# First loads split over two issuing engines, and attention's first two score tiles placed inside the last value unit

## The chip, the cores and the metric

The kernel runs on one core of a Trainium2 chip. The metric is the device time of one execution in microseconds (us); the lower the better. Three runs of the kernel before took 1822.64, 1822.76 and 1823.33 us, so the median is 1822.76. One more execution was profiled. The profile gives times from the first instruction's start and names engines: PE is the matrix engine (PEld its weight loads), DVE is VectorE, ACT is ScalarE, POOL is GpSimd, SP is SyncE, which here only issues DMAs. A "q" behind an engine's name means its issuing sequencer.

## The reference

With x of shape (1, 2048, 1024), 32 heads of 32 channels, and everything in 32-bit floats:

```
def _A_ref(x, wqkv, wo):
    q, k, v = split(x @ wqkv)                       # 32 heads, 32 channels
    p = softmax(einsum("bhqd,bhkd->bhqk", q, k) * 32 ** -0.5)
    return merge_heads(einsum("bhqk,bhkd->bhqd", p, v)) @ wo

def _B_ref(x, w_q, k1, k2, u, v):                   # 64 experts, the best one per head
    q1, q2 = halves(einsum("nd,dhc->nhc", x, w_q))
    e = argmax(q1 @ k1.T) * 8 + argmax(q2 @ k2.T)   # per token and head
    return sum over heads of gelu(x . u[e]) * v[e]  # the softmax over one candidate is 1

g = sigmoid((x * gate_w).sum(-1))
return g * _A_ref(x, wqkv, wo) + (1 - g) * _B_ref(x, w_q, k1, k2, u, v)
```

## The kernel before, in words

Large products run as sums of rounded parts: an operand is split into a high part (ACT copies it, rounded: `hi_of`, or line 95 of `split`) and a low part (DVE subtracts the high part from the operand: line 96), and three products, high by high, high by low and low by high, are summed. Most of them also use a scheme with seven block products P1 to P7 where plain blocks would need eight; one such product is 12 matmuls into one PSUM bank (four steps over the inner dimension, three pairs of parts each). PSUM has eight banks per core, called `bk0` to `bk7` here.

The stages follow each other on PE, whose order is the order of the code; no scheduler moves anything (`tc.manual_schedule()`), and every engine works through its own list in that order, waiting on semaphores where an operand or a buffer is not ready.

1. Queries and keys (0 to 364 us). The first 128 columns of keys and of queries for the first 1024 tokens are done plainly, in eight steps kc of 128 input channels, 12 matmuls each (`plain_mm`, line 291). Step kc needs 128 rows of x for 1024 tokens and 128 x 128 blocks of two weights, called A and S in the profile. The code calls the loads of weights `load_w0(k0, k1, queues)`: columns k0 to k1 in units of 128, one DMA for each of the two weights, each on the queue named. `load_x(p, kc, pieces)` loads the 128 rows of step kc in that many DMAs; the rows of steps 0 to 3 lie in the raw tile that the profile calls `xh`. Before the first step, eight matmuls of an identity tile (line 409) run on PE. After step 3 the gate's small products follow (line 191).
2. The router of the expert part (364 to 453 us).
3. Values. Two passes for the last four tiles of 128 tokens (453 to 497 us), and then six value units of two tiles each (`values_unit`, 497 to 615 us), each with the seven products; the last unit takes them in the order P1, P7, P5, P6, P3, P2, P4. DVE assembles the results: after P6 it does four adds in a row, u2 = c1 + P6, u3 = u2 + P7, u2 = u2 + P5, u5 = u3 + P5; after P3, u2 = u2 + P3; after P2, c1 = c1 + P2; after P4, u3 = u3 + P4. A bank is free once the last add that reads it is done. In the last unit the products lie in these banks: P1 bk6, P7 bk7, P5 bk0, P6 bk1, P3 bk2, P2 bk3; P4 goes to a bank `o` in a new pool that takes the place of bk7 once the eight banks' pool is closed.
4. Attention (615 to 1641 us). For each head and each tile kt of 128 keys, four matmuls of 512 queries each give scores in seven banks used in turn, the ring (line 1322); ACT writes exp of them to a tile P (line 1332); four matmuls with the values add to the head's output (line 1343). Tiles go in pairs: PE does the scores of one pair and then the value products of the pair before. DVE sums P over the tiles for the softmax's denominator; four tiles of a head (three of the last) are summed by accumulating DMAs of POOL instead, into a tile `accd` (`SUMS` names the tiles kt that do so; ACT writes the first of them straight into `accd`). The scores of head 0's first tile are taken out of this loop: `first_scores`, lines 1219 to 1229, issues them in the last value unit, between P2 and P4, into the banks bk5, bk6, bk0 and bk1, and exp of them (line 1229) follows on ACT.
5. The output product with the expert part added, and the stores (1641 to 1821 us).

DMAs that SP and ACT issue carry one of eight semaphores in turn, and an issue waits until the DMA before it with the same semaphore has landed.

Of the kernel before, what the change touches and what calls it, by code (L numbers as in the profile page):

```python
# [18 lines left out]
H = 32  # L19
# [12 lines left out]
def gated_mha_peer_kernel(ctx, tc, xT, wqkv, wv, wo, wq, k12, ug, v, out):  # L32
# [8 lines left out]
    nc = tc.nc  # L41
# [33 lines left out]
    def dma(dst, src, queue=nc.sync):  # L75
        a, b = (ap.bitcast(F32) if ap.dtype == F32R else ap for ap in (dst, src))
        return queue.dma_start(a, b)
# [92 lines left out]
    def load_x(p, kc, pieces=1):  # L170
        rows, t0 = slice(kc * 128, (kc + 1) * 128), TOK0[p]
        if kc < HC:
            n = 1024 // pieces
            for i in range(pieces):
                dma(XR["ra"][:, kc, i * n:(i + 1) * n], xT[rows, t0 + i * n:t0 + (i + 1) * n])
        else:
            for i, name in enumerate(("B21", "B22")):
                dma(XR[name][:, kc - HC, :], xT[rows, t0 + i * 512:t0 + (i + 1) * 512])
# [102 lines left out]
    b0, prod_no = {}, [0]  # L281
# [88 lines left out]
    def load_w0(k0, k1, queues=(nc.sync, nc.sync)):  # L370
        for w, queue in enumerate(queues):
            dma(w0[:, w, k0:k1], wqkv[w * 8, :, k0 * 128:k1 * 128].rearrange("p (k m) -> p k m", m=128),
                queue)

    def split_w0(k0, k1):
        ki, k = divmod(k0, HC)
        for w in range(2):
            hi, lo = AW[PLAIN[w, ki]]
            split(hi[:, k:k + k1 - k0], lo[:, k:k + k1 - k0], w0[:, w, k0:k1])
# [11 lines left out]
    for name in ("B11", "B12", "B21", "B22"):  # L391
        X[name] = x_parts(PASS[0][name], None, xp)

    load_w0(0, 1, (nc.scalar, nc.sync))
    load_x(0, 0, 2)
    load_w0(1, 2)
    load_x(0, 1)
    split_w0(0, 1)
    split_x(0)
    load_w0(2, 4)  # L400
# [264 lines left out]
    wl_, wh_, pools = [], [], []  # L665
# [239 lines left out]
    tp = Pool("tp", side="right")  # L905
# [64 lines left out]
    def tt(out, a, b, op=OP.add):  # L970
        nc.vector.tensor_tensor(out=out, in0=a, in1=b, op=op)
# [108 lines left out]
    def load_x_raw(u):  # L1080
        dma(x_raw[u % 2], xT[:, u * W:(u + 1) * W].rearrange("(k p) m -> p k m", p=128))
# [63 lines left out]
    def values_unit(u):  # L1145
        last = u == NU - 1
        c1, u2, u3, u5 = (work[k] for k in ("c1", "u2", "u3", "u5"))
        if last:
            free = x_raw[(u + 1) % 2].rearrange("p k m -> p (k m)").rearrange("p (a m) -> p a m", m=512)
            c1, u2, u3, u5 = (free[:, k] for k in range(4))  # L1150
        order = (("P1", "P2", "P3", "P7", "P5", "P6", "P4") if u == 0 else
                 ("P1", "P7", "P5", "P6", "P3", "P2", "P4") if last else
                 ("P1", "P7", "P5", "P6", "P2", "P3", "P4"))
        p, done = {}, set()

        def out(j, half, t, queue=nc.sync):
            dma(VD[half][(2 * u + j) * 128:(2 * u + j + 1) * 128, :], t, queue)

        for k, name in enumerate(order):
            if last and name == "P4":  # L1160

                nonlocal pso
                ps1.close()
                pso = Pool("pso", space=PSUM, side="right")
            p[name] = hv.product(name, bank=pv_bank if last and name == "P4" else None)
            if last and name == "P2":
                first_scores()
            if name == "P1":
                nc.scalar.activation(c1, p[name], AF.Copy)
                hv.rows(x_raw[(u + 1) % 2])  # L1170
                if u + 2 < NU:
                    load_x_raw(u + 2)
            if name == "P6":
                tt(u2, c1, p["P6"])
                tt(u3, u2, p["P7"])
                tt(u2, u2, p["P5"])
                tt(u5, u3, p["P5"])
                out(1, 1, u5)
            if "P6" in p:
                if "P2" in p and "C11" not in p:  # L1180
                    p["C11"] = tt(c1, c1, p["P2"])
                    out(0, 0, c1)
                if "P3" in p and "C12" not in p:
                    p["C12"] = tt(u2, u2, p["P3"])
                    out(0, 1, u2)
            if name == "P4":
                tt(u3, u3, p["P4"])

                out(1, 0, u3, nc.gpsimd if last else nc.sync)

            if u + 1 < NU:
                if k == (4 if u == 0 else 0):
                    hv.parts("A11")
                    for s in ("S3", "S1", "S2", "S4"):
                        hv.sums(s)
                    done = {"P1"}
                if k >= 5 or u > 0:
                    for q in ("P7", "P5", "P6", "P2", "P3", "P4"):
                        if q in p and q not in done:
                            hv.parts(hv.FACTORS[q][0])  # L1200
                            done.add(q)
            if 1 <= u <= HC:
                if k == 0:
                    load_early(u - 1)
                if k == 3:
                    sums_early()
                for j in {4: (0,), 5: (1,), 6: (2, 3)}.get(k, ()):
                    split_early(u - 1, j)

    P, pools = {}, {}  # L1210

    def p_tile(h, kt):

        i = pools["next"] % 8
        pools["next"] += 1
        P[h, kt] = pools["left" if i >= 4 else "right"].tile([128, S], F32, name=f"P{i}")
        return P[h, kt]

    def first_scores():

        tp.close()
        pools.update(right=Pool("ppr", side="right"), next=0)
        K, Q = Z
        pt = p_tile(0, 0)
        for qc, i in enumerate((5, 6, 0, 1)):
            ps = ps1.tile([128, 512], F32, name=f"bk{i}")
            c = slice(qc * 512, (qc + 1) * 512)
            nc.tensor.matmul(ps, K[:98, :128], Q[:98, c], start=True, stop=True)
            nc.scalar.activation(pt[:, c], ps, AF.Exp, scale=SCALE)

    def pv_bank():
# [49 lines left out]
    def ring_banks(n):  # L1281
        i = [(ring_no[0] + k) % NB for k in range(n)]
        ring_no[0] += n
        return i
# [26 lines left out]
    def scores(tiles):  # L1311


        n = NQ * len(tiles)
        banks = ring_banks(n)
        cuts = {1} | set(range(NQ, n + 1, NQ)) | {c for c in range(1, n) if banks[c] == 0}
        cuts |= {c + 2 for c in range(NQ, n, NQ) if not cuts & {c + 1, c + 3}}
        c0 = 0
        for c, i in enumerate(banks):
            (h, kt), qc = tiles[c // NQ], c % NQ  # L1320
            K, Q = KQ[h % 2]
            on_ring(nc.tensor.matmul(ring[:, i, :], K[:98, kt * 128:(kt + 1) * 128],  # L1322
                                     Q[:98, qc * 512:(qc + 1) * 512], start=True, stop=True), i)
            if c + 1 not in cuts:
                continue
            q0, m = c0 % NQ, c + 1 - c0
            if q0 == 0 and kt == SUMS[h == H - 1][0]:
                P[h, kt] = ACCD[h] = wk.tile([128, S], F32, name="accd")
            elif q0 == 0:
                p_tile(h, kt)  # L1330
            i -= m - 1
            on_ring(nc.scalar.activation(  # L1332
                P[h, kt][:, q0 * 512:(q0 + m) * 512].rearrange("p (a m) -> p a m", a=m),
                ring[:, i:i + m, :], AF.Exp, scale=SCALE), *range(i, i + m))
            c0 = c + 1
# [12 lines left out]

    SUMS = (1, 3, 8, 12), (2, 4, 6)

    def rowsum(ps, *srcs):
        for src in srcs:
# [3 lines left out]
                                       start=(src is srcs[0]), stop=(src is srcs[-1]))  # L1358

    def presum(h, kt):  # L1360
        sums = SUMS[h == H - 1]
        if kt == 0 or kt == sums[0] or (h == H - 1 and kt >= NT - 2):
            return
        if kt in sums:
            nc.gpsimd.dma_start(ACCD[h], P[h, kt], accum_op=OP.add)  # L1365
            return
        if kt == 1 + (sums[0] == 1):
            if h > 0:
                ACC[h] = wk.tile([128, S], F32, name="acc")
            nc.vector.tensor_add(ACC[h], P[h, 0], P[h, kt])  # L1370
        else:
            nc.vector.tensor_add(ACC[h], ACC[h], P[h, kt])  # L1372
# [97 lines left out]
    for k in range(2 * KC):  # L1470
        c = slice(k % 2 * D // 2, (k % 2 + 1) * D // 2)
# [10 lines left out]
    for b0 in range(0, (H + 1) * NT, BT):  # L1482
        if b0 > H * NT:
            break
        now = [divmod(k, NT) for k in range(b0, b0 + BT)] if b0 < H * NT else []
        if now:

            scores(now[b0 == 0:])
        for k in range(b0 - BT, b0):
            if k >= 0:  # L1490
                pv(*divmod(k, NT))
        for k in range(b0, b0 + BT):
            for f, a in todo.pop(k, []):
                f(*a)
            if now:
                presum(*now[k - b0])
# [278 lines left out]
```

## Time and profile before

| | |
|---|---|
| median of three runs | 1822.76 us |
| the profiled execution, whole | 1822.43 us |
| its span, first to last instruction | 1820.6 us |
| PE's granted clock | 1.0 of full speed |
| PE busy | 1813.5 us, 100% of the span |
| DVE, ACT, POOL busy | 1461.6, 1313.0, 227.7 us |
| DMA engines, mean | 190 GB/s |

A row of the timeline gives the start in us, the time from the first start to the last end of instructions merged into it, the engine and line, the operation, output<-inputs, the shape, and the count; a bracket at its end gives the engine's idle time before it and what ended it. A row of the table of waits gives who waited for whom, the total in us, how often, and the longest. A row of the chain of waits gives start, length, and what was done or waited for there. Ends of matmuls are modelled, so a matmul's length in these rows is longer than the distance to the next one's start; the text works with starts.

### The profile page before, as it was taken

The numbers are of one execution on the slowest core, as the hardware profiler recorded it, in microseconds if no ns is written. First come the engines' busy times: TensorE is split into PE (matmuls) and PEld (weight loads), VectorE is DVE, ScalarE is ACT, GpSimd is POOL, SyncE is SP. The second block draws the span as 40 slices with busy tenths as digits, with TensorE's granted clock in tenths as the row PEclk, the third lists the DMA queues.
The fourth block names the chain that finished last, engine by engine and source line by source line (L and its number), as shares of the span: only waits on it lengthen the run. The fifth ranks groups of instructions, "written<-read, shape, count | busy, mean of one in ns | idle before, by whom it ended". The sixth has DMA issues, their size and how long they took to land.

```text
span 1820.6 us, 26391 instructions
## 1 busy us (share of the span) xinstructions
PE 1813.5 (100%) x10077; PEld 1100.2 (60%) x10077; DVE 1461.6 (80%) x1258; ACT 1313.0 (72%) x1716; POOL 227.7 (13%) x351
## 2 busy tenths in 40 slices
PE   9999999999999999999999999999999999999999
PEld 6777777788888644444444444444444444447887
DVE  8865966789967888888888888888888888897674
ACT  6545544522333699999999999999999999994221
POOL 1222222244101100000000000000000000000000
PEclk9999999999999999999999999999999999999999
DMA  7888698660267778777778878888787778866641
GB/s 272 281 276 273 216 295 289 196 220 13 81 231 247 223 166 183 156 170 165 169 171 174 185 160 179 171 172 181 164 185 167 163 164 181 186 149 240 256 157 58
DMA packets 117072, 345.23 MB, mean 190 GB/s; under 512 B 16112, under 2 KB 49552, under 8 KB 96016
## 3 DMA queue, kind: packets, MB, share of 16 engines
q1 hardware_dynamic: 87752, 196.35, 36.6%
q0 software_dynamic: 27888, 145.00, 34.5%
q10 hardware_dynamic: 1304, 2.17, 0.3%
q8 instruction: 80, 1.31, 0.3%
q14 instruction: 48, 0.39, 0.1%
HBM read 171.76 MB, written 72.36 MB: 134 GB/s over the span
## 4 chain that ended last, share of the span: by engine, by line
PE 99%; DMA 0%; ACT 0%; SPq 0%; DVE 0%; issue 0%; DVEq 0%; ACTq 0%
PE ring L1322 29%; PE o L1343 26%; PE bk L303 15%; PE pa L965 6%; PE bk L965 6%; PE bk L726 5%; PE pa L1525 2%; PE bk L984 2%; PE bk L291 2%; PE bk L342 2%; PE ring L1356 1%; PE pa L1532 1%; PE bk L191 0%; DMA xh<-in_xT 0%; PE bk L359 0%; ACT P L1332 0%
## 5 line engine op out<-in xcount | busy, mean ns | idle before, releaser
L1332 ACT ACTIVATE P<-ring 128x1024 f32<-128x1024 f32 (+2 forms) x1031 | 913.0, 984 | 13.3 <-DMA accd<-P 0.2
L1372 DVE TENSOR_TENSOR acc<-acc,P 128x2048 f32<-128x2048 f32 x319 | 730.9, 2291 | 74.4 <-ACT P L1332 47.9
L1343 PE MATMUL o<-P,V 128*32 128x512 f32 x3840 | 464.9, 599 | 0.0
L1322 PE MATMUL ring<-Q,K 98*128 98x512 f32 x1024 | 271.8, 407 | 0.1
L1322 PE MATMUL ring<-z,z 98*128 98x512 f32 x1020 | 270.5, 407 | 0.6 <-ACT accd L1332 0.6
L1322 PEld LDWEIGHTS ring<-Q,K 98*128 98x128 f32 x1024 | 182.4, 188 | 143.5 <-ACT P L1332 73.6
L1322 PEld LDWEIGHTS ring<-z,z 98*128 98x128 f32 x1020 | 181.7, 188 | 142.1 <-ACT P L1332 72.3
L1343 PEld LDWEIGHTS o<-P,V 128*32 128x32 f32 x3840 | 99.2, 109 | 223.1 <-issue 214.4
L1365 POOL DMA_DIRECT2D accd<-P x95 | 81.5, 858 | 928.6 <-ACT P L1332 349.5
L1370 DVE TENSOR_TENSOR acc<-P,P 128x2048 f32<-128x2048 f32 x32 | 73.4, 2292 | 72.9 <-ACT P L1332 72.9
L303 PE MATMUL bk<-xh,A 128*128 128x512 f32 x336 | 82.8, 396 | 0.0
L303 PE MATMUL bk<-xh,S 128*128 128x512 f32 x336 | 81.3, 393 | 0.0
L303 PE MATMUL bk<-xl,S 128*128 128x512 f32 x336 | 80.1, 391 | 0.0
L136 ACT ACTIVATE hi<-u 128x512 fp32r<-128x512 f32 x42 | 26.6, 632 | 71.5 <-issue 37.0
L303 PEld LDWEIGHTS bk<-xh,A 128*128 128x128 f32 x336 | 62.1, 188 | 23.7 <-issue 5.9
L1375 DVE TENSOR_TENSOR acc<-acc,accd 128x2048 f32<-128x2048 f32 x32 | 73.1, 2284 | 0.0
L303 PEld LDWEIGHTS bk<-xl,S 128*128 128x128 f32 x336 | 62.8, 188 | 16.2 <-issue 2.5
L303 PEld LDWEIGHTS bk<-xh,S 128*128 128x128 f32 x336 | 62.5, 188 | 14.5 <-issue 1.7
L1332 ACT ACTIVATE accd<-ring 128x1024 f32<-128x1024 f32 (+2 forms) x64 | 62.3, 1034 | 1.8 <-PE ring L1322 1.7
L965 PE MATMUL pa<-woh,acc 128*128 128x512 f32 x192 | 62.2, 390 | 0.0
L513 DVE TENSOR_TENSOR u<-u,bk 128x512 f32<-128x512 f32 x70 | 46.6, 682 | 10.5 <-DMA wpd<-u 6.2
L730 ACT ACTIVATE xu<-bk 128x64 f32<-128x64 f32 x16 | 3.6, 222 | 61.4 <-PE bk L726 61.4
(303 smaller groups left out, 2208.5 us busy)
## 6 DMA issues: line engine op xcount, KB each, us to landing
accd<-P POOLq DMA_DIRECT2D x95, 1024.0 KB, 7.8
wqt<-in_wq SPq DMA_DIRECT2D x64, 512.0 KB
wraw<-in_wqkv SPq DMA_DIRECT2D x28, 512.0 KB
kdh<-hi POOLq DMA_DIRECT2D x32, 256.0 KB, 6.2
kdl<-lo POOLq DMA_DIRECT2D x32, 256.0 KB, 6.7
qdh<-hi POOLq DMA_DIRECT2D x32, 256.0 KB, 6.1
qdl<-lo POOLq DMA_DIRECT2D x32, 256.0 KB, 5.9
z<-kdh SPq DMA_DIRECT2D x32, 256.0 KB
```

The lines of the kernel that those rows point to most:

```text
L291: nc.tensor.matmul(b0[w, n], AW[PLAIN[w, ki]][a][:, k, :], X[f"B{ki + 1}{n + 1}"][b][:, k, :], start=first, stop=last)
L303: nc.tensor.matmul(ps, a[i][:, k, :], b[j][:, k, :], start=(k == 0 and i == j == 0), stop=(k == HC - 1 and i == 1))
L513: nc.vector.tensor_tensor(out=out, in0=a, in1=b, op=OP.add)
L726: nc.tensor.matmul(ps, x_part(a, t // 4, kc)[:, tok], b, start=first, stop=last)
L965: nc.tensor.matmul(ps, self.a[a][i][:, k, :], self.b[b][j][k], start=(not first and k == 0 and i == j == 0), stop=(k == HC - 1 and i == 1))
L1322: on_ring(nc.tensor.matmul(ring[:, i, :], K[:98, kt * 128:(kt + 1) * 128], Q[:98, qc * 512:(qc + 1) * 512], start=True, stop=True), i)
L1332: on_ring(nc.scalar.activation(P[h, kt][:, q0 * 512:(q0 + m) * 512].rearrange("p (a m) -> p a m", a=m), ring[:, i:i + m, :], AF.Exp, scale ...
L1343: nc.tensor.matmul(O[h][32 * qc:32 * qc + 32, :], Vt[g][:, kt, 32 * j:32 * j + 32], p[:, qc * 512:(qc + 1) * 512], start=(kt == 0), stop=( ...
L1365: nc.gpsimd.dma_start(ACCD[h], P[h, kt], accum_op=OP.add)
L1370: nc.vector.tensor_add(ACC[h], P[h, 0], P[h, kt])
L1372: nc.vector.tensor_add(ACC[h], ACC[h], P[h, kt])
L1375: nc.vector.tensor_add(ACC[h], ACC[h], ACCD[h])
```

## The change

Two places are changed.

At the start, ACT issues both weights for steps 0 and 1 in two DMAs of 128 x 256; before, ACT issued the first weight of step 0 and SP the second, and SP issued both weights of step 1 in two more. SP starts with x: steps 0 and 1 in two pieces of 512 tokens each, four DMAs of 128 x 512; before, step 1 was one DMA of 128 x 1024. The splits stay as they were, in the same order.

In the last value unit `first_scores` is called twice: after P3 for tile 0, into the banks bk5, bk6, bk7, bk0, and after P2 for tile 1, into bk1, bk2, bk5, bk6. The loop of attention then leaves its whole first pair out and begins with tiles 2 and 3. Tile 1 of head 0 thus lies in an ordinary P tile; the tiles of head 0 that the accumulating DMAs sum become 2, 4, 8 and 12, where they were 1, 3, 8 and 12. `SUMS` is now looked up by head.

```
-    load_w0(0, 1, (nc.scalar, nc.sync))
+    load_w0(0, 2, (nc.scalar, nc.scalar))
     load_x(0, 0, 2)
-    load_w0(1, 2)
-    load_x(0, 1)
+    load_x(0, 1, 2)
     split_w0(0, 1)
     split_x(0)
     load_w0(2, 4)
...
             p[name] = hv.product(name, bank=pv_bank if last and name == "P4" else None)
-            if last and name == "P2":
-                first_scores()
+            if last and name in ("P3", "P2"):
+                first_scores(*((0, (5, 6, 7, 0)) if name == "P3" else (1, (1, 2, 5, 6))))
...
-    def first_scores():
+    def first_scores(kt, banks):
 
-        tp.close()
-        pools.update(right=Pool("ppr", side="right"), next=0)
+        if kt == 0:
+            tp.close()
+            pools.update(right=Pool("ppr", side="right"), next=0)
         K, Q = Z
-        pt = p_tile(0, 0)
-        for qc, i in enumerate((5, 6, 0, 1)):
+        pt = p_tile(0, kt)
+        for qc, i in enumerate(banks):
             ps = ps1.tile([128, 512], F32, name=f"bk{i}")
             c = slice(qc * 512, (qc + 1) * 512)
-            nc.tensor.matmul(ps, K[:98, :128], Q[:98, c], start=True, stop=True)
+            nc.tensor.matmul(ps, K[:98, kt * 128:(kt + 1) * 128], Q[:98, c], start=True, stop=True)
             nc.scalar.activation(pt[:, c], ps, AF.Exp, scale=SCALE)
...
-            if q0 == 0 and kt == SUMS[h == H - 1][0]:
+            if q0 == 0 and kt == SUMS[h][0]:
...
-    SUMS = (1, 3, 8, 12), (2, 4, 6)
+    SUMS = {h: (1, 3, 8, 12) for h in range(H)} | {0: (2, 4, 8, 12), H - 1: (2, 4, 6)}
...
-            scores(now[b0 == 0:])
+            if b0:
+                scores(now)
```

SP's list at the start, before: the weights (`wraw`) of steps 0 and 1 stand between the pieces of x.

```order
L77 DMA wraw<-in_wqkv 128x128
L77 DMA xh_135<-in_xT 128x512 x2
L77 DMA wraw<-in_wqkv 128x128 x2
L77 DMA xh_135<-in_xT 128x1024
L77 DMA wraw<-in_wqkv 128x256 x2
L77 DMA xh_135<-in_xT 128x1024
```

Now, from the same place on:

```order
L77 DMA xh_135<-in_xT 128x512 x4
L77 DMA wraw<-in_wqkv 128x256 x2
L77 DMA xh_135<-in_xT 128x1024
L77 DMA wraw<-in_wqkv 128x512 x2
L77 DMA xh_135<-in_xT 128x1024
```

Three weight DMAs have left SP's list ahead of step 2's x, and one x DMA is added. On ACT's list, the first operations before:

```order
L77 DMA wraw<-in_wqkv 128x128
L95 ACT_TABLE_LOAD
L95 ACTIVATE A_138<-wraw 128x128
L95 ACTIVATE S_140<-wraw 128x128
L95 ACTIVATE xh_142<-xh_135 128x512
```

and now:

```order
L77 DMA wraw<-in_wqkv 128x256 x2
L95 ACT_TABLE_LOAD
L95 ACTIVATE A_138<-wraw 128x128
L95 ACTIVATE S_140<-wraw 128x128
L95 ACTIVATE xh_142<-xh_135 128x512
```

One more issue stands ahead of ACT's table load. PE's list at the end of the last value unit, before; the first row is P6, then P3 (`bk2`) and P2 (`bk3`), the scores of tile 0 (line 1228), and the first matmuls of P4 (`o`):

```order
L965 MATMUL bk1_5394<-xh1_4581,xh0_4576 128x512 x12
L965 MATMUL bk2_5412<-xl1_4043,xh0_4576 128x512 x12
L965 MATMUL bk3_5427<-xl2_4221,a1_4452 128x512 x12
L1228 MATMUL bk5_5445<-z1_4908,z0_4907 128x512
L1228 MATMUL bk6_5448<-z1_4908,z0_4907 128x512
L1228 MATMUL bk0_5451<-z1_4908,z0_4907 128x512
L1228 MATMUL bk1_5454<-z1_4908,z0_4907 128x512
L965 MATMUL o_5463<-xl3_4589,vo_4586 128x512 x2
```

and now (the code has one line less ahead, so line 965 is 964):

```order
L964 MATMUL bk1_5393<-xh1_4580,xh0_4575 128x512 x12
L964 MATMUL bk2_5411<-xl1_4042,xh0_4575 128x512 x12
L1228 MATMUL bk5_5429<-z1_4907,z0_4906 128x512
L1228 MATMUL bk6_5432<-z1_4907,z0_4906 128x512
L1228 MATMUL bk7_5435<-z1_4907,z0_4906 128x512
L1228 MATMUL bk0_5438<-z1_4907,z0_4906 128x512
L964 MATMUL bk3_5443<-xl2_4220,a1_4451 128x512 x12
L1228 MATMUL bk1_5457<-z1_4907,z0_4906 128x512
L1228 MATMUL bk2_5460<-z1_4907,z0_4906 128x512
L1228 MATMUL bk5_5463<-z1_4907,z0_4906 128x512
L1228 MATMUL bk6_5466<-z1_4907,z0_4906 128x512
L964 MATMUL o_5475<-xl3_4588,vo_4585 128x512 x2
```

Tile 0's scores have moved ahead of P2, with bk7 and bk0 as their third and fourth bank, and tile 1's have come from the ring to the place after P2. On the ring, 8 matmuls follow P4 where there were 12. DVE's list keeps its order.

2 lines of the change are left out of this document (1 added, 1 removed).

## The prediction, made before the changed kernel ran

> **What bounds the kernel now.** I read the table of waits first, for PE over the whole span. This is all of it but a last row of 0.3 us:
>
> ```profile
> PE bk L409 <- DVE ident L91: 1.4, 1, 1.4
> PE bk L291 <- ACT xh L95: 1.0, 2, 0.8
> PE ring L1322 <- ACT accd L1332: 0.6, 1, 0.6
> ```
>
> PE is the bound nearly everywhere: in 1820.6 us it stands still for 3.3 us that the profile can see. The change moves PE's work and removes none of it, so it can win only what PE loses in waiting at the two places it touches, the first steps (second row) and the hand-over to attention (third row). Next I read the chain of waits over the first 25 us:
>
> ```profile
> 0.76 0.40 SPq L77
> ...
> 2.62 0.45 SPq L77
> ...
> 3.11 5.99 DMA xh<-in_xT
> ...
> 9.12 0.64 ACT xh L95
> ...
> 10.40 0.69 DVE xh L96
> ...
> 11.13 7.82 PE bk L291 x33
> ```
>
> The kernel's whole length hangs on the x of step 1: SP issues it at 3.11, as its sixth DMA, it lands 5.99 us later, its high and low parts are made, and PE runs without a break from 11.13. PE's own timeline shows what is lost before that:
>
> ```profile
> 1.40 3.78 PE L409 MATMUL bk<-ident 128*128 128x128 f32 x16 [1.40 <-DVE ident L91]
> 5.35 1.22 PE L291 MATMUL bk<-xh,A 128*128 128x512 f32 x2 [0.17 <-ACT xh L95]
> 8.62 0.40 PE L291 MATMUL bk<-xh,S 128*128 128x512 f32 x1
> 13.34 1.53 PE L291 MATMUL bk<-xh,A 128*128 128x512 f32 x6
> 16.07 1.52 PE L291 MATMUL bk<-xh,A 128*128 128x512 f32 x6
> ```
>
> Step 0 begins at 5.35 and its last matmul at 8.62; step 2 begins at 13.34 and step 3 at 16.07. An undisturbed step of 12 matmuls thus takes 16.07 - 13.34 = 2.73 us, 0.23 each. Step 1 could begin at 8.62 + 0.23 = 8.85 and step 2 at 11.58; the loss in step 1 is 13.34 - 11.58 = 1.76 us.
>
> **The first loads.** When they are issued and used:
>
> ```profile
> 1.22 0.89 SPq L77 DMA_DIRECT2D xh<-in_xT  x2
> 4.54 0.43 SPq L77 DMA_DIRECT2D xh<-in_xT  x1
> 1.21 1.28 ACT L95 ACT_TABLE_LOAD   x1 [1.21 <-PEq L1767]
> 3.35 0.31 ACT L95 ACTIVATE A<-wraw 128x128 fp32r<-128x128 f32 x1 [0.85 <-DMA wraw<-in_wqkv]
> 4.67 0.63 ACT L95 ACTIVATE xh<-xh 128x512 fp32r<-128x512 f32 x1 [0.81 <-DMA xh<-in_xT]
> 5.61 0.63 ACT L95 ACTIVATE xh<-xh 128x512 fp32r<-128x512 f32 x1 [0.31 <-DMA xh<-in_xT]
> 11.35 1.15 ACT L95 ACTIVATE xh<-xh 128x512 fp32r<-128x512 f32 x2 [0.46 <-DMA xh<-in_xT]
> ```
>
> An issue takes SP about 0.46 us (two in 0.89). Step 0's x is issued first now, at 0.76 for 1.22. With its own 4.67 - 1.22 = 3.45 us to landing ACT could start on it at 4.21 and end by 4.84, but the identity matmuls end at 1.40 + 3.78 = 5.18, so PE gains 0.17 at most. ACT pays for its second issue: the table load ends 0.45 later, at 2.94, before the weights were there in any case (3.35). The weights of step 0 now carry step 1's with them and the second of them goes out one issue later, some 0.45; they have until 4.21. I cost the start of step 0 at nothing; if the weights came 1 us late, step 0 would begin near 5.8.
>
> Step 1's x is the third and fourth of SP's issues, at 1.68 and 2.14, where the whole was at 3.11. What it gains in landing no row shows; three prices bound it. Had it the spacing of step 0's two pieces, 5.61 - 4.67 = 0.94 each, the halves would be there at 6.1 and 7.0. With the whole's 5.99 us each, the later half lands at 8.13. If the DMA engines are the limit, as many bytes as before stand ahead of its end (the same weights and the same x), and only SP's earlier start counts: 9.10 - 0.46 = 8.64. I take 8.13, the row of the load itself. The second half's high part is then ready at 8.13 + 0.65 = 8.8 and its low part 0.7 later, at 9.5; PE, beginning at 8.85, wants them as its second and fourth matmul, at 9.08 and 9.54. No wait is left in step 1.
>
> What is late next is step 2's x. DVE, after ACT, makes its low parts:
>
> ```profile
> 12.01 1.29 DVE L96 TENSOR_TENSOR xh<-xh,xh 128x512 fp32r<-128x512 f32 x2 [0.26 <-ACT xh L95]
> ```
>
> The second is done at 13.30; PE used it as the fourth matmul of step 2, at 13.34 + 3 x 0.23 = 14.02. That is 0.72 of slack. SP's issue of this x moves up by two places (six DMAs stand ahead of it, where there were eight), 0.92, so step 2 can move by 0.72 + 0.92 = 1.64 before it waits. I take **1.65 us gained**, all kept, since PE runs without a break afterwards and the loads and splits of later steps move with these. The bounds: 1.76 + 0.17 = 1.93 if everything lands early enough; 1.05 if step 1's x lands at 8.64 (its last low part at 10.04 is wanted as the fourth matmul, which was at 11.13); nothing or a loss if the weights' double size delays both.
>
> **The hand-over.** PE's timeline from the start of P3 to the first value products of attention:
>
> ```profile
> 605.97 2.89 PE L965 MATMUL bk<-xl,xh 128*128 128x512 f32 x12
> 608.69 2.96 PE L965 MATMUL bk<-xl,a 128*128 128x512 f32 x12
> 611.49 1.09 PE L1228 MATMUL bk<-z,z 98*128 98x512 f32 x4
> 612.42 2.96 PE L965 MATMUL o<-xl,vo 128*128 128x512 f32 x12
> 615.22 1.99 PE L1322 MATMUL ring<-z,z 98*128 98x512 f32 x8
> 617.85 1.20 PE L1322 MATMUL ring<-z,z 98*128 98x512 f32 x4 [0.64 <-ACT accd L1332]
> 618.98 1.07 PE L1343 MATMUL o<-P,V 128*32 128x512 f32 x8
> ```
>
> From P2's start to the first value products it is 618.98 - 608.69 = 10.29 us: 2.80 for P2, 0.93 for the scores, 2.80 for P4, 3.76 on the ring, where PE waits 0.64 for exp to free a bank: twelve matmuls, seven banks. With tile 1 taken out, eight are left; the eighth needs the first one's bank, which ACT frees while PE fills the others. The first eight of before ended 1.99 us after they began; I take 2.10 to the next start. Without any wait the new order would take 0.93 + 2.80 + 0.93 + 2.80 + 2.10 = 9.56 us, a gain of 0.73.
>
> It adds a wait, though. Tile 0's scores now want bk7 and bk0 directly after P3, and these hold P7 and P5 until DVE's adds have read them: the second of the four adds after P6 frees bk7, the fourth bk0. DVE is behind:
>
> ```profile
> 599.94 2.14 DVE L971 TENSOR_TENSOR xl<-xl 128x512 f32<-128x512 f32 x3 [1.12 <-DMA xl<-in_wo]
> 606.81 1.28 DVE L96 TENSOR_TENSOR xl<-xl,xu 128x512 fp32r<-128x512 f32 x2
> 608.01 0.68 DVE L971 TENSOR_TENSOR xw<-xw,bk 128x512 f32<-128x512 f32 x1
> 608.72 0.69 DVE L971 TENSOR_TENSOR xw<-xw,bk 128x512 f32<-128x512 f32 x1
> 610.05 1.28 DVE L971 TENSOR_TENSOR xw<-xw,bk 128x512 f32<-128x512 f32 x2
> ```
>
> P6 ends when P3 starts, near 606, but DVE is still splitting weights for the output product (606.81) and begins the adds at 608.01. The second ends at 609.41, the fourth at 610.05 + 0.68 = 610.73. PE comes to bk7 at 608.69 + 2 x 0.23 = 609.15 and waits 0.3 us; it comes to bk0 one matmul later and waits until 610.77, in all 1.39 us more than 608.69 + 3 x 0.23 = 609.38. P2 starts at 611.0 instead of 609.62. The sum for the hand-over is 9.56 + 1.39 = 10.95 us against 10.29: **0.66 lost**. Queued behind the waiting matmul stand P2 and everything else on PE.
>
> The rest of this part costs nothing. Exp of tile 0 falls in ACT's idle time, and bk5 and bk6 are long free when tile 1 wants them after P2. The first load of V stands on SP's queue behind the store of c1 + P2, which moves with P2's end from 611.5 to 613.8:
>
> ```profile
> 612.82 6.80 SPq L77 DMA_DIRECT2D V<-vd  x4
> ```
>
> It would go out near 615.1 and is wanted at 608.69 + 10.95 = 619.64, 4.5 us later; as many bytes of x took 3.45. ACT does the same exps, four of them earlier; DVE's adds and POOL's accumulations for head 0 keep their number. The ring starts one tile later, so its banks' wrap falls elsewhere in every pair; it goes through all places in any case.
>
> **The sum.** -1.65 + 0.66 = -0.99. The profiled execution took 1822.43 us (1820.6 of span and 1.83 around it), 0.33 below the median; it would take 1821.44, and the median 1822.76 would become **1821.8 us**. That is 0.05%, and about 0.2% (3.65 us) is what a measurement of this kernel can tell from no change.
>
> **The rivals.** (B) The loads are limited by the DMA engines, not by the issue. Then step 1's x lands at 8.64, the first part gains 1.05, the sum is -0.39: 1822.4. For it: between step 0's second piece (5.61) and step 1's x (9.10) nothing but the two small weights landed. Against: those halves of x were 0.94 apart. The Trainium skill, "DMA: Bandwidth & Descriptors", section "Issuing engines are not separate DMA queues", says that DMAs started by different engines run on the same 16 DMA engines and interleave, so that a second issuer only saves issuing time; that is this rival, and by it 1822.4 is the time; the trace here does not settle it.
>
> (C) DVE is not behind when PE comes, or its adds come before the splits: then the hand-over gains 0.73, and the sum is -2.38: 1820.4. Against it stands DVE's unbroken row of work from 599.94 on.
>
> (D) Slower. DVE's backlog began with a load of `wo` for which DVE waited until 599.94. If that load's time does not move with PE, PE arrives 1.65 us earlier at the same adds, and the wait on bk0 takes back the whole first gain: the sum is +0.66, 1823.4. Each further us by which the adds come later against PE costs one; the total is a loss as soon as they come 0.99 us later against P3 than in this trace. For it: the load, its splits and the store that frees its buffer make a loop of their own. Against: the loop starts from events on PE in the units before. With a weak first part (1.05) it would be 1824.
>
> (E) Something slower by more than 3.65 us that no row here shows, such as later stages that lose their slack once PE runs 1.6 us ahead. (F) A gain above 3.65 us: the two places hold 1.93 + 0.73 = 2.66 at most, so it would have to come from elsewhere.
>
> **Chances.** Forecast 42%, B 17, C 10, D 20, E 7, F 4. The range reaches from C to D with a weak first part, with some 0.2 us around for the spread of runs: 1820.2 to 1824.2. It leaves out E, F and the edges of C and D. Within 0.2% lie the forecast, B, C and D: 0.89; faster is F, 0.04; slower E, 0.07.
>
> **What would show it.** In the changed kernel's profile step 1's x should reach ACT before 8.2, and step 2 of the first product begin near 11.7; if it begins after 12.3, B holds. At the end of the last value unit, P3's scores (line 1228) should stop before the fourth matmul with a wait for DVE's adds of about 1.1 us, and the ring's wait for ACT (0.6 us) be gone. A wait well above 1.4 us there means D, none means C. The prediction is wrong if PE waits in a stage that neither part touches.

## The result, and the profile after

The changed kernel is slower. Over 20 runs each, its median is 1826.45 us and that of the kernel before 1823.35 us; the ratio is 1.0014, with a 95% interval of 1.0008 to 1.0021. By the ratio some 2.6 us were lost; the medians lie 3.1 us apart. The profiled execution took 1826.02 us, with a span of 1824.3 us (before 1820.6). The forecast had been 1821.8, in a range from 1820.2 to 1824.2.

PE's table of waits, of the changed kernel, without a last row of 0.4 us:

```profile
PE ring L1322 <- ACT P L1332: 1.9, 2, 1.7
PE bk L291 <- ACT xh L95: 1.8, 1, 1.8
PE bk L408 <- DVE ident L91: 1.4, 1, 1.4
PE bk L1228 <- DVE xw L970: 0.5, 1, 0.5
```

The wait between P3 and P2 that the prediction added is there (last row shown), and the ring's wait for `accd` (0.6 us) is gone. But PE now waits 1.8 us in one piece in the first steps, where it had waited 1.0, and a wait of 1.7 us for exp is new. PE's timeline at the start:

```profile
7.01 0.73 PE L291 MATMUL bk<-xh,A 128*128 128x512 f32 x2 [1.83 <-ACT xh L95]
...
9.87 1.52 PE L291 MATMUL bk<-xh,A 128*128 128x512 f32 x6
...
12.59 1.52 PE L291 MATMUL bk<-xh,A 128*128 128x512 f32 x6
```

Step 0 starts at 7.01, 1.66 us later than before (5.35); steps 1 and 2 then follow without a gap, and step 2 begins at 12.59, 0.75 us earlier than before (13.34). ACT's timeline says what step 0 waited for:

```profile
5.18 0.31 ACT L95 ACTIVATE A<-wraw 128x128 fp32r<-128x128 f32 x1 [2.21 <-DMA wraw<-in_wqkv]
6.13 0.31 ACT L95 ACTIVATE S<-wraw 128x128 fp32r<-128x128 f32 x1 [0.64 <-DMA wraw<-in_wqkv]
6.34 1.14 ACT L95 ACTIVATE xh<-xh 128x512 fp32r<-128x512 f32 x2
...
7.79 1.14 ACT L95 ACTIVATE xh<-xh 128x512 fp32r<-128x512 f32 x2
```

The weights of step 0 land at 5.2 and 6.1, where ACT had them at 3.35. Both pieces of step 0's x stand behind them on ACT's list, though they had landed by then, since ACT does not wait at 6.34.

PE's timeline from P3 into the first head:

```profile
605.28 2.88 PE L964 MATMUL bk<-xl,xh 128*128 128x512 f32 x12
608.00 0.86 PE L1228 MATMUL bk<-z,z 98*128 98x512 f32 x3
609.30 0.50 PE L1228 MATMUL bk<-z,z 98*128 98x512 f32 x1 [0.45 <-DVE xw L970]
...
618.06 1.92 PE L1343 MATMUL o<-P,V 128*32 128x512 f32 x16
...
635.54 1.91 PE L1322 MATMUL ring<-z,z 98*128 98x512 f32 x7
639.16 0.50 PE L1322 MATMUL ring<-z,z 98*128 98x512 f32 x1 [1.71 <-ACT P L1332]
639.59 2.80 PE L1343 MATMUL o<-P,V 128*32 128x512 f32 x16
642.32 2.83 PE L1322 MATMUL ring<-z,z 98*128 98x512 f32 x8
645.08 1.92 PE L1343 MATMUL o<-P,V 128*32 128x512 f32 x16
```

Until 618.06, the first value products, PE is ahead of the kernel before (618.98) by 0.92 us. Between 635.54 and 645.08 this is lost and more. The scores from 635.54 on take until 639.59, 4.05 us where 2.04 is usual, and the next two groups take 2.73 and 2.76 us where they take 1.86 and 2.06 elsewhere: after its wait of 1.71 us PE ran at a lower clock. The view by stretches has it (the stretch, its length, PE's busy time with its instructions, the granted clock, the DMA engines' share and GB/s):

```profile
640.00:644.00 4.00, 4.00 (x20) 0.57 0.96 197
```

The record of the granted clock shows 0.5 for 3.41 us from 640.49. What the wait was for stands in the chain of waits of the same stretch, and the wait itself in ACT's timeline:

```profile
623.64 14.78 DMA accd<-P
...
638.51 0.61 ACT P L1332
```

```profile
638.51 3.84 ACT L1332 ACTIVATE P<-ring 128x512 f32<-128x512 f32 x5 [2.48 <-DMA accd<-P]
```

It is the accumulating DMA of tile 4. Exps go into eight P buffers in turn (`p_tile`), so the exp of tile 12 writes where tile 4 lay and must wait until that DMA has read it. ACT came there at 636.03 and went on at 638.51. In the kernel before, the same place belonged to tiles 3 and 11, and the margin was already gone. Its rows are the issue on POOL's timeline, the wait on ACT's, and the DMA's time to landing from the view on `accd` between 612 and 630 us:

```profile
621.82 0.90 POOL L1365 DMA_DIRECT2D accd<-P  x1 [4.88 <-PE ring L1322]
```

```profile
635.39 5.61 ACT L1332 ACTIVATE P<-ring 128x1024 f32<-128x1024 f32 x6 [0.16 <-DMA accd<-P]
```

```profile
DMA to landing us min/median/max: 13.5/13.5/13.5
```

Against the profile of before, PE stands at -0.76 us after the first steps, at -0.9 after the hand-over, and at +2.67 at 645 us; over the other heads another 0.9 us builds up in steps of some 0.03 (0.25 in a second profile of this kernel, and 0.10 the other way in the profile with the hand-over alone). The cause of that last part is open.

### The profile page after: what moved, and what is told of

Its sections match the earlier page's. It is cut to its first block, busy times and chain, and to the rows that moved or that the text cites. A ratio compares the mean times of both kernels' runs of the same rounds, so it can differ in the third digit from the quotient of the medians.

```text
span 1824.3 us, 26392 instructions
## 1 busy us (share of the span) xinstructions
PE 1814.5 (99%) x10077; PEld 1099.0 (60%) x10077; DVE 1461.6 (80%) x1258; ACT 1314.3 (72%) x1718; POOL 229.0 (13%) x351
## 4 chain that ended last, share of the span: by engine, by line
PE 64%; DMA 1%; ACT 0%; issue 0%; DVE 0%; DVEq 0%; ACTq 0%
PE ring L1322 28%; PE o L1343 25%; PE pa L964 6%; PE pa L1526 2%; PE ring L1356 1%; DMA accd<-P 1%; PE pa L1533 1%; ACT P L1332 0%; PE o L1356 0%; ACT z L1440 0%; DVE osb L970 0%; DVEq L1772 0%; ACTq L1440 0%; ACTq L1332 0%
## 5 line engine op out<-in xcount | busy, mean ns | idle before, releaser
L1332 ACT ACTIVATE P<-ring 128x512 f32<-128x512 f32 (+2 forms) x1028 | 911.7, 986 | 16.6 <-DMA accd<-P 2.5
```

Source lines behind the costliest of these rows:

```text
L1332: on_ring(nc.scalar.activation(P[h, kt][:, q0 * 512:(q0 + m) * 512].rearrange("p (a m) -> p a m", a=m), ring[:, i:i + m, :], AF.Exp, scale ...
```

## The experiments

Ratios are to runs of the kernel before on the same chip, with their 95% intervals.

**The two parts apart.** First the loads alone:

```
-    load_w0(0, 1, (nc.scalar, nc.sync))
+    load_w0(0, 2, (nc.scalar, nc.scalar))
     load_x(0, 0, 2)
-    load_w0(1, 2)
-    load_x(0, 1)
+    load_x(0, 1, 2)
```

> The first loads alone, the hand-over as before. Theory one (tile 4's accumulating DMA holds a P buffer, and only the hand-over brings that): PE starts step 0 late, near 7.0 us, behind the weights, then runs steps 1 and 2 without a break, and is 0.76 us ahead of the kernel before from there to the end; no wait of PE in attention but the 0.6 us of before; about 0.8 us faster than before, ratio 0.9996. Rival (PE's earlier arrival in attention makes the new stall, whatever the hand-over): ACT waits 1 us or more for an accumulating DMA in head 0 here too, and the time is 1 to 3 us above before.

Median 1822.61 us against 1822.48, ratio 0.9997 (0.9988 to 1.0006): no gain that can be measured, and no wait of 1 us in attention. But the profiled execution is 0.67 us behind before after the first steps, and not 0.76 ahead, so this trace does not test an earlier arrival of PE in attention. Two below do, those with the small weights and with twelve identity matmuls: with the old hand-over they reach the first value products 1.83 and 1.33 us ahead of before and have no such wait. So the earlier loads do not make the stall. PE is late in the trace here though step 0 starts even earlier than in the changed kernel:

```profile
6.81 1.22 PE L291 MATMUL bk<-xh,A 128*128 128x512 f32 x2 [1.62 <-ACT xh L95]
...
8.68 0.63 PE L291 MATMUL bk<-xh,A 128*128 128x512 f32 x1
9.11 0.63 PE L291 MATMUL bk<-xh,S 128*128 128x512 f32 x1
...
11.27 1.55 PE L291 MATMUL bk<-xh,A 128*128 128x512 f32 x6
```

Step 0 takes 4.46 us here (6.81 to 11.27), against 2.86 in the profile above (7.01 to 9.87): until 10.3 a matmul takes 0.43 us (8.68 to 9.11), and the record of the granted clock has full clock from 10.28 on. The run times lie apart too: 5 of the 11 at 1821.36 to 1821.54, the others at 1822.61 and more.

Then the hand-over alone, with the first loads as before:

```
-    load_w0(0, 2, (nc.scalar, nc.scalar))
+    load_w0(0, 1, (nc.scalar, nc.sync))
     load_x(0, 0, 2)
-    load_x(0, 1, 2)
+    load_w0(1, 2)
+    load_x(0, 1)
```

(a diff against the changed kernel, as are those that follow unless something else is said).

> The hand-over alone, the first loads as before. Theory one: PE reaches the first value products 0.2 us earlier or up to 0.7 us later than before; then, in head 0, ACT waits 1 to 2.5 us for the accumulating DMA of tile 4 before the exp of tile 12, PE waits 0.5 to 1.7 us behind it, and PE's granted clock may fall to half for some 3 us; 1 to 4 us slower than before. Rival (the earlier arrival from the loads is needed for the stall): no such wait, time within 0.7 us of before.

1824.94 us against 1822.48, ratio 1.0010 (1.0001 to 1.0019). In its profile ACT waits 1.42 us for tile 4's DMA and 1.45 more for the next one, and PE 1.7 us behind them in three pieces; its clock does not fall:

```profile
638.89 7.50 ACT L1333 ACTIVATE P<-ring 128x512 f32<-128x512 f32 x9 [1.42 <-DMA accd<-P]
647.84 1.94 ACT L1333 ACTIVATE P<-ring 128x512 f32<-128x512 f32 x2 [1.45 <-DMA accd<-P]
```

PE comes to the first value products 0.53 us later than before here, not earlier. The loss belongs to the hand-over, not to its meeting with the loads.

**Is it tile 4's DMA?** Tile 4 goes to DVE, and nothing else is changed:

```
-    SUMS = {h: (1, 3, 8, 12) for h in range(H)} | {0: (2, 4, 8, 12), H - 1: (2, 4, 6)}
+    SUMS = {h: (1, 3, 8, 12) for h in range(H)} | {0: (2, 8, 12), H - 1: (2, 4, 6)}
```

> The changed kernel, but tile 4 of head 0 is summed by DVE and not by an accumulating DMA (three tiles of that head are summed by DMAs, not four). Theory one: no DMA holds tile 12's buffer, ACT's wait of 2.5 us and PE's of 1.7 us go, the granted clock stays at 1.0, and 3 to 3.6 us of the changed kernel's time come back: 0.5 to 1.7 us faster than before, about 1822. Rival (ACT or the ring's banks set the stall, not that DMA): the wait stays near 638 us and the time stays 2 to 3 us above before. Third: DVE, with one sum more, becomes late in its place, and P buffers wait for DVE by a microsecond or more.

1823.26 us against 1822.48, ratio 1.0003 (0.9994 to 1.0012). ACT and PE wait for no DMA in the first head, and DVE carries the sum without becoming late: the stall hung on that DMA. The expected gain of 0.5 to 1.7 us over before did not come. PE is 0.90 us ahead of before until P3 and 0.25 behind from the first value products on: what is left is the wait between P3 and P2, larger here than in the profile above. The timelines of PE and DVE in this kernel:

```profile
605.07 2.88 PE L964 MATMUL bk<-xl,xh 128*128 128x512 f32 x12
607.79 0.63 PE L1228 MATMUL bk<-z,z 98*128 98x512 f32 x2
609.12 0.50 PE L1228 MATMUL bk<-z,z 98*128 98x512 f32 x1 [0.70 <-DVE xw L970]
610.44 0.51 PE L1228 MATMUL bk<-z,z 98*128 98x512 f32 x1 [0.82 <-DVE xw L970]
```

```profile
599.59 2.15 DVE L970 TENSOR_TENSOR xl<-xl 128x512 f32<-128x512 f32 x3 [1.69 <-DMA xl<-in_wo]
...
607.66 1.40 DVE L970 TENSOR_TENSOR xw<-xw,bk 128x512 f32<-128x512 f32 x2
```

and of DVE in the changed kernel:

```profile
598.46 2.15 DVE L970 TENSOR_TENSOR xl<-xl 128x512 f32<-128x512 f32 x3 [0.45 <-DMA xl<-in_wo]
...
606.52 3.32 DVE L970 TENSOR_TENSOR xw<-xw,bk 128x512 f32<-128x512 f32 x5
```

DVE's adds begin 2.59 us after P3 here (607.66 - 605.07) and 1.24 in the changed kernel's profile (606.52 - 605.28). By the prediction's own working the fourth add ends 2.72 after the first begins and PE would want it 2.72 + 0.69 after P3's start, so the wait is that distance less 0.65: 1.94 and 0.59. Measured by starts it is 610.44 - 607.79 - 0.69 = 1.96 and 609.30 - 608.00 - 0.69 = 0.61. With the trace of before the distance had been 2.04, and the wait 1.39. In the three traces the adds begin 8.06 to 8.07 us after DVE got its load of `wo`, at 599.94, 598.46 and 599.59. Against before, PE comes to P3 0.69 and 0.90 us earlier in the last two, and the load 1.48 and 0.35: the landing of that load, which does not follow PE, makes the difference.

A second way to move the DMA was to let it take tile 6:

```
+    ... {0: (2, 6, 8, 12), ...
```

> The changed kernel, but the first accumulating DMA of head 0 takes tile 6 and not tile 4: as many sums on DVE and on the DMAs as in the changed kernel. Theory one: the DMA goes out near 627 us, as the loads of head 1 are all issued; its buffer is wanted near 640 us by tile 14; if it lands at 638 to 640, little or nothing is waited, and 2 to 3.6 us come back against the changed kernel. If the landing is 13 to 15 us after the issue whatever the loads do, ACT waits 0 to 2 us at tile 14 in place of tile 12. Rival (not that DMA): nothing changes against the changed kernel.

1826.61 us against 1822.48, ratio 1.0020 (1.0011 to 1.0029): no better. The wait is not at tile 14 but one DMA later. The DMAs of a head add into one tile and go one after the other; tile 6's landed at 640.70, tile 8's went out at 641.24 and held its buffer until 648.08, when tile 16, the first of the next head, had wanted it for 2.14 us:

```profile
648.16 1.94 ACT L1332 ACTIVATE P<-ring 128x512 f32<-128x512 f32 x2 [2.14 <-DMA accd<-P]
```

So a later start is no repair; the landing must come earlier.

**Why does the landing take so long?** With tile 4 on DVE, tile 8's DMA went out at 631.88 and landed 8.1 us later; tile 4's had taken 14.8. What runs beside it are the loads of the next head, on the same DMA engines. In the changed kernel SP issues them late:

```profile
613.75 8.90 SPq L77 DMA_DIRECT2D V<-vd  x4
622.70 0.96 SPq L77 DMA_DIRECT2D K<-kdh  x2
```

The third load of V needs the last values, which POOL stores at 617.33, and waits for that store; K and Q of head 1 stand behind it. Against the first value products they go out 3.96 us later than before: 4.64 behind (622.70 - 618.06) for 0.68 (619.66 - 618.98). The store's issue makes 1.85 of this. The rest is that the store itself lands 4.4 us after its issue, where it took 2.3 before. The DMA views between the store's issue and its landing, first of before (616.4 to 618.7), then of the changed kernel (617.33 to 621.73), a queue with its packets, MB and share of the 16 engines, and the store with its KB and us to landing:

```profile
vd<-xw POOLq DMA_DIRECT2D x1, 256.0 KB, 2.3
```

```profile
q8 instruction: 1, 0.02, 2.6%
...
vd<-xw POOLq DMA_DIRECT2D x1, 256.0 KB, 4.4
```

One packet of 16 KB of the queue that the profile calls instruction lies among the store's: 2.6% of 16 engines over 4.4 us is 1.8 us of one engine. By the single records it ran from 618.45 to 620.26; the store's last four data packets on one engine began at 620.24, and all its other data was through by 619.26. In the ten profiles with this order of loads, such a packet begins 0.2 to 0.6 us after the first value products of attention, also before (619.34, with the products at 618.98). There the store goes out 2.58 us ahead of the products and is through when the packet comes; now it goes out 0.73 ahead (617.33, 618.06), because only eight matmuls stand on the ring between them, with no wait. The store takes 2.3 us in all four with the old hand-over and 4.1 to 4.4 in all six with the new one. In the three profiles with the loads in another order such a packet begins 2.7 to 4.2 us after the products. That the packet fetches PE's code for them is what its moment in the ten suggests, and that it holds the store back is read from these traces; no run tested either. The next run takes SP's queue out of the way of that store:

```
-    for i in range(4):
+    for i in (0, 1, 3):
         load_v(0, i)
     nc.vector.memset(KQ[1][0][96:98, :].bitcast(F32), 1.0)
     load_head(1)
+    load_v(0, 2)
```

> The changed kernel, but the third load of V (which waits for POOL's store of the last values) is issued behind the loads of head 1 and not ahead of them. Theory (the store lands 2 us later than before because a 16 KB instruction-fetch packet sits on one DMA engine at that moment; behind the waiting third load SP's queue holds head 1's loads, and those then delay tile 4's accumulating DMA): the loads of head 1 go out near 615 to 620 us, the accumulating DMA lands by 632, ACT's and PE's waits at tile 12 go, the time falls by 2.5 to 3.5 us against the changed kernel, to within 1 us of before. Rival (the accumulating DMA takes 13 to 15 us anyway, or goes out too late whatever the loads do): ACT still waits 1 to 2.5 us near 636 and nothing is won. Third: V's third quarter comes too late for tile 8, and PE waits for it near 634.

1822.50 us against 1822.57, ratio 0.9998 (0.9989 to 1.0007). Against the changed kernel's 1.0014 that is the whole loss. SP's timeline and POOL's:

```profile
615.41 1.56 SPq L77 DMA_DIRECT2D V<-vd  x3
618.00 0.80 SPq L77 DMA_DIRECT2D K<-kdh  x2
...
627.68 1.79 SPq L77 DMA_DIRECT2D V<-vd  x2
```

```profile
625.31 0.90 POOL L1366 DMA_DIRECT2D accd<-P  x1 [5.78 <-ACT P L1333]
```

Head 1's loads go out from 618.0, 4.7 us earlier (1.73 us ahead of the first value products, for 4.64 behind them), and tile 4's DMA, still out at the same distance behind the products, lands at 634.03, after 8.7 us. ACT and PE wait for no DMA. The store now takes 8.7 us itself, among those loads, and V's third quarter goes out at 627.68; PE has no wait for it either. The landing of tile 4's DMA, and with it the stall, hung on the loads beside it.

**The wait between P3 and P2.** Tile 4 on DVE again, and tile 0's scores in banks that need only DVE's second add:

```
-                first_scores(*((0, (5, 6, 7, 0)) if name == "P3" else (1, (1, 2, 5, 6))))
+                first_scores(*((0, (5, 6, 4, 7)) if name == "P3" else (1, (1, 2, 5, 6))))
```

> The changed kernel with tile 4 on DVE, as in the run before, and tile 0's scores in bk5, bk6, bk4, bk7 and not bk5, bk6, bk7, bk0: PE then waits for DVE's second add after P6 alone, not for the fourth. Theory: the wait of 0.4 to 1.5 us between P3 and P2 falls by 0.8 to 1.1 us, to 0 to 0.6; about 0.9 us faster than the kernel with tile 4 on DVE alone, ratio to before 0.9994 to 0.9998. Rival (the wait is not on those banks, or is taken again by P4 or the ring): the first value products begin no earlier against P3 than in that kernel.

1822.33 us against 1822.57, ratio 0.9994 (0.9985 to 1.0003). Against before on the same chip the median is 0.24 us under, where with tile 4 on DVE alone it was 0.78 above; the two intervals overlap. From the first score to P2 it is 1.16 us (0.93 without any wait):

```profile
609.64 1.32 PE L1228 MATMUL bk<-z,z 98*128 98x512 f32 x4
610.80 2.96 PE L964 MATMUL bk<-xl,a 128*128 128x512 f32 x12
```

DVE's adds begin 2.08 us after P3 in this trace (609.00 - 606.92). By the working above the old banks would have made a wait of 1.43; 0.23 is left.

**The first loads.** The kernel before, with step 0's weights first and small, as they were, step 1's on ACT, and x in four pieces:

```
     load_w0(0, 1, (nc.scalar, nc.sync))
     load_x(0, 0, 2)
-    load_w0(1, 2)
-    load_x(0, 1)
+    load_w0(1, 2, (nc.scalar, nc.scalar))
+    load_x(0, 1, 2)
```

> The first loads otherwise, the hand-over as before: step 0's two weights go out first as before, one column block each; step 1's two, one column block each, from ACT; x in four pieces on SP. Theory (the double-size weights, on the same 16 DMA engines as the x that now starts beside them, held step 0 back): step 0 starts near 5.35 as before, step 1 follows it without more than 0.3 us of wait, and PE is 1.3 to 1.8 us ahead of the kernel before, but for what the clock's step to full speed does; 1 to 1.8 us faster than before. Rival (ACT's third issue or the clock eats it): step 0 again near 7 us, gain 0.5 us or less.

1821.35 us against 1822.57, ratio 0.9993 (0.9984 to 1.0002). Step 0 starts at 5.81, step 1 at 8.70, step 2 at 11.49, 1.85 us earlier than before:

```profile
5.81 0.74 PE L291 MATMUL bk<-xh,A 128*128 128x512 f32 x2 [0.79 <-ACT xh L95]
...
8.70 1.57 PE L291 MATMUL bk<-xh,A 128*128 128x512 f32 x6
...
11.49 1.53 PE L291 MATMUL bk<-xh,A 128*128 128x512 f32 x6
```

So in this execution x in pieces is worth what had been forecast, though the interval of the runs reaches 1. What took it away in the change are step 0's weights, which are twice as large there and have x issued beside them from the first moment; no run parts these two.

The last question was the half clock. The first loads of the change alone, with four identity matmuls more, so that PE works through the pause:

```
-    for i in range(8):
+    for i in range(12):
         nc.tensor.matmul(b0[1, 1][:, :128], ident, ident, start=True, stop=True)
```

> The first loads of the change alone, with 12 identity matmuls ahead of step 0 and not 8, so that PE works until about 7.0 us and does not stand still for 1.6 us before step 0. Theory (PE's clock goes to full speed only after some 3 us of unbroken work; the pause sends it back in about half of the executions, and step 0 and part of step 1 then run at half speed until about 10 us): the slow group of runs (1822.6 and more) goes, nearly all come at 1821.3 to 1821.9, and in the profile each matmul of step 0 takes 0.23 us at the latest from 8.2 us on. Rival (the clock comes at a random moment whatever PE does): two groups as before, median near 1822.5.

1821.69 us against 1822.83, ratio 0.9992 (0.9983 to 1.0001); all 11 runs lie between 1820.99 and 1822.54, with no gap among them. None is as late as 1822.61, where six of the 11 with the loads alone lay, as the theory had it, though the intervals of the two kernels overlap. In the profile step 0 runs at full clock from its start; this alone does not speak for the four matmuls, since the clock was granted at 5.20 us, when eight would only just have ended:

```profile
1.40 4.74 PE L408 MATMUL bk<-ident 128*128 128x128 f32 x24 [1.40 <-DVE ident L91]
6.45 0.73 PE L291 MATMUL bk<-xh,A 128*128 128x512 f32 x2 [0.31 <-ACT xh L95]
```

**Together**, the small weights, the banks bk5, bk6, bk4, bk7, the order of the loads of V and tile 4 on DVE:

> All repairs together: the small weights, the banks bk5, bk6, bk4, bk7 for tile 0, the third load of V behind head 1's, tile 4 on DVE. By the theory the gains add: 1.3 to 1.8 us from the loads and 0.2 to 0.9 from the hand-over, 1.5 to 2.5 us faster than before, ratio 0.9986 to 0.9992. If one repair does not hold, its share is missing and its wait is seen at its place.

1820.63 us against 1822.57, ratio 0.9991 (0.9982 to 1.0000). At the first value products PE is 2.68 us ahead of before in its profile: 2.09 from the loads and 0.59 from the hand-over, where 0.34 of the wait between P3 and P2 is left. With nine identity matmuls for eight:

> All repairs, with 9 identity matmuls and not 8, so that PE's pause of 0.4 us before step 0 is filled. Theory on the clock: the group of runs near 1822.4 goes and the median stays at 1820.4 to 1820.8, 0.0010 to 0.0015 under before. Rival: two groups as without it.

1821.08 us against 1822.83, ratio 0.9989 (0.9980 to 0.9998): faster than before beyond its interval, and the two versions can't be told apart. Ten of the eleven runs lie between 1820.37 and 1821.84; without the ninth, seven lay at 1820.28 to 1820.72 and four at 1822.35 and more. In the profile with nine, step 0 still began at half clock, until 7.08 us.

**The changed kernel once more:**

> The changed kernel once more, with a second profile. Theory: ACT again waits for tile 4's accumulating DMA near 636 us, 1 to 2.5 us, PE 0.5 to 1.7 us behind it, and the wait between P3 and P2 is again between 0.4 and 1.5 us; about 1.0014 times before. If the stall is missing in this profile while the time is the same, the stall is not what the change costs.

1825.82 us against 1822.83, ratio 1.0017 (1.0008 to 1.0026). ACT waits 2.0 us for tile 4's DMA (14.3 us to landing) and 1.0 for the next, PE 1.9 us in three pieces, and the clock stays up there. After the first steps PE is 0.77 us behind before in this execution, at half clock until 10.4. The stall is in all three profiles that have the hand-over as it was changed, the fall of the clock in one.

## Why the prediction was wrong

**The step that failed** is "the rest of this part costs nothing", with "POOL's accumulations for head 0 keep their number". Their number stayed, but the second moved from tile 3 to tile 4. The buffer that it reads was to be free 13.4 us after its issue before (621.82 to 635.23) and 12.4 now (623.64 to 636.03), since the DMA adds into tile 2's P, which PE must first have read in the value products from 621.98 on. And it landed later, 14.8 us for 13.5. With the 0.16 us that were missing before, these two make up ACT's 2.48. The row that tells this stood in the profile of before: ACT's wait of 0.16 us for that same DMA. Such a wait means that the slack is nothing there, and that each us of delay becomes waiting on ACT; in the three other profiles with the old hand-over the DMA landed after 12.6 to 13.0 us, a slack of 0.4 to 0.8. PE lost 2.5 to 3.6 us in the two profiles of the kernel, with its waits behind ACT and, in one, the fall of the clock. The prediction had named this sign itself: it is wrong "if PE waits in a stage that neither part touches".

**The first loads**: the step "I cost the start of step 0 at nothing" failed. The forecast looked at issues: ACT's second issue is 0.45 us, and there was time until 4.21. The weights of step 0 became 1.8 and 2.8 us later, since twice their bytes and x, issued at the same moment, came over the same engines. This is what rival B had said of the DMA engines, applied to step 1's x, where it was not needed: those halves landed in time (ACT takes the second at 8.31 without a wait, ahead of B's 8.64), near the price of 8.13, and step 1 follows step 0 without a gap. Step 2 began at 12.59, past the 12.3 that was to show B, but because step 0 was late. In the seven profiles with these loads step 2 begins 0.75 and 0.88 us earlier than before in two, and 0.45 to 0.97 later in the five whose step 0 ran at half clock; the median of the loads alone does not move. The bound "nothing or a loss if the weights' double size delays both" was the case. With small weights 1.85 us came in one profile.

One more step was wrong and did no harm, by luck. Step 2's x was to go out 0.92 us earlier, and it went out 0.63 later, at 5.17 for 4.54:

```profile
5.17 0.33 SPq L77 DMA_DIRECT2D xh<-in_xT  x1
```

It is the ninth DMA of SP and ACT, so by the turn of eight semaphores it shares one with the first weight, and it waited for that weight to land (ACT starts on it at 5.18). It was there by 10.12 all the same, 1.23 us earlier than before (11.35), so step 2 did not wait.

**The hand-over**: mechanism and working held; the wait is the distance between P3 and DVE's adds less 0.65 us, to within 0.02, in all six traces with these banks. Its size was that of one execution: forecast 1.39, measured 0.59 to 1.96 in the six, and 0.61 in the profile of the change. Rival D had named what sets it, the load of `wo` that does not move with PE, and had it stand still; it moves from one execution to the next. The ring's wait went, as forecast. In the profile of the change PE goes from 0.69 us ahead at P3 to 0.92 at the first value products: 0.23 gained where 0.66 lost had been forecast.

**The chances**: what happened lies nearest to rival E, "later stages that lose their slack", at 7%, with a loss of less than its 3.65 us and without its condition, a lead of PE: the stall is there with the hand-over alone. The prediction had priced the waits that the diff touches, and not those that stood at zero beside it.

## What to carry to other kernels

Before a change, list the waits near zero as well as the long ones, DMAs that free a buffer first of all: a buffer in turn of eight that comes free 0.16 us late has no room for a DMA moved by one tile. When loads are moved between issuing engines, count the bytes that stand ahead of the first one wanted, not the issues. A DMA that waits on a queue holds all that stands behind it, so what waits for the last store goes last.

## What the runs showed of the hardware

Packets of the queue that the profile calls instruction share the DMA engines with the kernel's own. Beside the last store one of 16 KB ran for 1.6 to 1.9 us (0.9 to 1.5 where it came after the store), and the store's last four packets began as it ended: 4.1 to 4.4 us for 256 KB instead of 2.3, in all six kernels whose store fell at that moment and had no other loads beside it.

A pause of PE can cost more than itself. In seven profiles PE stood still for 1.5 to 1.8 us before step 0; in five of them its matmuls took twice their time until 9.9 to 10.7 us, in two only the pause was lost. In six with pauses of 0.8 us or less, full clock came by 7.1 us. After the 1.71 us in attention the clock was at 0.5 for 3.41 us; after waits of 0.4 to 1.5 us in three other profiles it stayed. The Trainium skill, "TensorE: Matmul & The Clock Gate", section "What's actually happening", has a window of 3.413 us that runs freely, by whose activity the clock is set to half or full; the 3.41 us here agree. The records of the granted clock agree too: in all 13 profiles each stretch of full clock is a whole number of 3.413 us, 186 and 346 in the changed kernel and 530 to 532 in the others. A free window would explain why the same pause costs 1.6 us more in one execution than in another (from step 0's start to step 2's it is 7.20 us with the loads alone and 5.58 in the changed kernel). In the two spared profiles full clock was granted at 5.17 and 5.61 us, before or early in the pause. In the other five the window that ended between 6.5 and 7.3 us held 1.3 to 1.8 us of standing still, and full clock came one window later.

The kernel before shows the same in its granted clock: of its 93 runs beside the experiments, 27 have a mean granted clock of 0.999 and took 1824.07 us or more, and the other 66, at 1.000, took 1823.41 or less. No profile of one of the 27 was kept, so where the clock falls in them is open.
